# A new fixed order of the instructions on all five engines, chosen with VectorE's two-SBUF-input additions and GpSimd's instructions excluding each other

## The chip, the cores and the metric

The kernel runs on one core of one Trainium2 chip. The metric is device time in microseconds (us), the median of several runs; lower is better. A core has five engines with an instruction queue each: TensorE (PE, matmuls; its weight loads are shown apart as PEld), VectorE (DVE), ScalarE (ACT), GpSimd (POOL) and SyncE (SP). Here SyncE does nothing but issue the DMA transfers, all of them on one queue.

## The reference

Two identical layers, each of linear attention and a gated MLP, on 2048 rows of width 512 (32 heads of 16, MLP width 1792):

```python
def _A_ref(x, wqkv, wo):
    q, k, v = (x @ wqkv).reshape(B, S, 3, H, Dh).transpose(2, 0, 3, 1, 4)
    phi = lambda t: jnp.where(t > 0, t + 1, jnp.exp(t)) + 1e-6
    pq, pk = phi(q), phi(k)
    kv = jnp.einsum("bhsd,bhse->bhde", pk, v)
    z = jnp.einsum("bhsd->bhd", pk)
    num = jnp.einsum("bhqd,bhde->bhqe", pq, kv)
    den = jnp.einsum("bhqd,bhd->bhq", pq, z)[..., None] + 1e-6
    return (num / den).transpose(0, 2, 1, 3).reshape(B, S, D) @ wo

def _B_ref(x, w1, w3, w2):
    return (silu(x @ w1) * (x @ w3)) @ w2

for _ in range(2):
    x = x + _A_ref(_layernorm(x), A_wqkv, A_wo)
    x = x + _B_ref(_layernorm(x), B_w1, B_w3, B_w2)
```

## The kernel before

All matmuls run on fp16 pairs: every operand is split into a high and a low fp16 part, and a product takes three passes (high by high, low by high, high by low; `PASSES`). Large products are done as seven half-size products with 256 columns (a Winograd form), whose banks in PSUM are called bb, ba and bc in the MLP, kb, kc and ka for the keys of layer 2, qb, qc and qa for its queries. In layer 1 the keys have a bank pk and the Gram matrix of the rows gt; po is an output bank.

**Rows and tiles.** The 2048 rows are 16 tiles of 128. For each tile, VectorE takes the moments (L909 and L910, `bn_stats` and `bn_aggr`), GpSimd computes scale and shift in four or five small operations (L917 to L921, among them the power L918), ScalarE normalises (L924), ScalarE writes the high part and GpSimd or VectorE the low part, and a DMA transposes the pair (L939, L1858; in layer 2 L1590 and L1593 for the seven-product form). A copy of the transposed rows is stored in HBM (L1875, L1594) and loaded back later (L1888, L1685) for the queries. The first two tiles are transposed by TensorE instead (`turn`, L2355); their low parts are L2361.

**Scale of the weights.** Before the first product, VectorE takes the largest absolute value of four pieces of the key weights (L789), reduces these (L805), spreads the result over all partitions by a small matmul (`pm_k`, L808) and makes a power of two of it (L810 to L821). ScalarE and VectorE then split the weights by it (L836 high, L837 low).

**Layer 2, keys.** `pair_turn` handles two tiles at once: ScalarE L1586 and GpSimd L1587 (high), GpSimd L1588 and L1589 (low), transpose L1590; ScalarE L1591, GpSimd L1592, transpose L1593; store L1594 of 896 KB to xt7_d. **Layer 2, queries:** ScalarE L1717 and VectorE L1718, L1732 to L1753 make the features, ScalarE L1759 and GpSimd L1760 split them, a DMA transposes them (L1769), and po matmuls read them. ScalarE L1634 takes a product out of PSUM. L947 is the line of nearly all matmuls (the helper `mm`).

**What sets the order.** The kernel is written as a program, and at its end `arrange()` gives every engine a fixed order: the table `ORDER` holds for each engine the numbers of its instructions, as traced, in the order in which they shall run. Each instruction then depends on its predecessor on its own engine:

```python
for engine, text in ORDER.items():
    at = []
    for part in text.split():
        first, _, last_ = part.partition("-")
        at.extend(range(int(first), int(last_ or first) + 1))
    for before, after in zip(at, at[1:]):
        tc.add_manual_dep(traced[engine][after], traced[engine][before].name, ...)
```

The semaphores between engines follow from the data. SyncE's DMAs use eight semaphores in turn, so each DMA is issued only after the one eight places ahead of it has landed.

Of the kernel before, what the change touches and what calls it, by code (L numbers as in the profile page):

```python
# [73 lines left out]
        "0-20 22-23 26-27 24 28 25 30 29 34 38-39 35-36 21 31-32 37 40-41 33 42-65 78-89 66-77 "  # L74
        "102-113 90-92 96-101 93-95 126-137 120-122 114-116 123-125 117-119 150-161 144-149 "
        "162-173 138-140 174-176 183-185 141-143 180-182 177-179 186-197 201-203 198-200 204-209 "
        "228-230 225-227 210-224 231-245 258-269 255-257 249-254 246-248 276-278 282-293 279-281 "
        "306 300-302 307 303-305 308-319 270-272 326-328 273-275 294-299 323-325 350-352 347-349 "
        "329-331 353-355 332-343 320-322 377-379 344-346 356-367 380-391 404 371-373 405-406 "
        "374-376 398-400 368-370 401-403 395-397 392-394 416-418 407-409 413-415 419-421 410-412 "  # L80
        "425-427 431 422-424 428-430 432-455 460-471 456-458 472-483 459 484-555 568-579 556-567 "
        "592-603 616-627 580-591 604-615 628-651 664-675 652-663 688-699 676-687 712-723 700-711 "
        "736-747 760-771 724-735 748-759 772-808 821-832 809-820 833-868 893-904 869-880 905-910 "
        "917-928 881-892 911-916 941-958 965-970 929-934 1001-1006 935-940 971-976 959-964 "
        "1007-1012 977-988 1109 1013-1018 1049-1054 1110-1111 1085-1090 1019-1024 1112 1117-1120 "
        "1055-1060 989-994 1121 1113 1122 1114 995-1000 1115-1116 1373-1374 1125 1381 1126 1375 "
        "1091-1096 1376-1377 1382 1378 1383 1123-1124 1379 1384-1385 1380 1386 1037-1042 1387 "
        "1389 1388 1127 1393 1390 1128-1130 1394 1025-1030 1043-1048 1031-1036 1395 1061-1066 "
        "1131 1217-1218 1097-1102 1132 1391 1396 1219 1067-1072 1103-1108 1220 1225-1226 "
        "1073-1078 1221 1227 1392 1397-1399 1157-1162 1079-1084 1228-1229 1222 1230-1231 1223 "  # L90
        "1405 1163-1168 1224 1232 1237 1133-1138 1145-1150 1400 1233-1234 1406 1238 1151-1156 "
        "1235 1407 1236 1408-1409 1193-1204 1401 1239 1402 1169-1174 1139-1144 1175-1180 "
        "1410-1411 1403-1404 1413-1415 1205-1210 1325 1240 1416 1326 1265-1270 1327 1211-1216 "
        "1181-1186 1421 1333 1412 1422-1424 1328 1425 1329 1334 1187-1192 1417-1418 1335-1336 "
        "1330-1332 1419 1301-1306 1341 1337 1307 1338 1420 1339 1426 1429-1430 1308-1312 1340 "
        "1431 1345 1432 1346 1433 1253-1264 1271-1276 1241-1246 1427 1434 1342 1435-1436 1441 "
        "1347 1428 1343 1348 1437-1438 1344 1247-1252 1439 1277-1288 1313-1318 1442-1443 "
        "1505-1506 1319-1324 1445-1450 1507 1444 1481-1486 1440 1289-1300 1451-1456 1508 1513 "
        "1349-1354 1509-1510 1769 1511 1514 1512 1777 1521 1515-1520 1522 1770-1771 1523 1772 "
        "1525 1773 1526 1361-1366 1778-1779 1524 1355-1360 1367-1372 1457-1462 1780 1774 1781 "  # L100
        "1613 1775 1782 1487-1492 1776 1783 1614-1615 1784-1785 1463-1468 1493-1498 1786-1787 "
        "1789 1788 1790 1616 1527 1791 1793 1792 1469-1474 1794 1475-1480 1499-1504 1617 1528 "
        "1621-1623 1553-1558 1624 1801 1625-1627 1529-1534 1618 1541-1546 1619 1559-1564 1620 "
        "1628 1535-1540 1629-1630 1547-1552 1795 1633-1634 1796-1798 1802-1805 1589-1594 1635 "
        "1799 1806-1807 1800 1809 1565-1570 1631 1810 1632 1808 1811-1812 1595-1606 1571-1576 "
# [64 lines left out]
        "3752-3757 3819-3820 3734-3745 3821-3822 3831 3823-3828 3857-3862 3791-3796 3803-3808 "  # L170
        "3817-3818 3833 3797-3802 3809-3814 3829 3835 3832 3848-3849 3834 3830 3836-3837 "
        "3863-3868 3838-3839 3844-3847 3840-3841 3856 3850 3842-3843 3854 3852 3855 3853 3851 "
        "3869-3874 3917-3918 3893-3898 3875-3880 3921-3924 3899-3904 3881-3886 3905-3910 "
        "3887-3892 3911-3916 3925-3926 3962-3967 3933 3919-3920 3931 3927-3928 3935 3929-3930 "
        "3968-3973 3998-4002 3937 3934 3950-3961 4034-4035 3938-3943 4042 4026-4029 4003 "
        "3944-3949 3932 3974-3979 4038-4039 4022-4023 3936 4024-4025 3980-3985 4030-4031 "
        "4067-4070 4036-4037 4081 4032-4033 4004-4009 3986-3991 4010-4015 4040-4041 4082 "
        "4088-4089 3992-3997 4071-4076 4083 4079-4080 4016-4021 4077-4078 4109-4114 4090-4091 "
        "4087 4084 4145-4150 4102 4092-4093 4115-4120 4055-4060 4151-4156 4061-4066 4094-4095 "
        "4100-4101 4121-4126 4085 4108 4104-4105 4157-4162 4103 4127-4132 4043-4048 4086 "  # L180
        "4169-4170 4163-4168 4133-4138 4096-4097 4139-4144 4049-4054 4098-4099 4106 4214-4219 "
        "4173-4174 4220-4225 4250-4255 4171-4172 4107 4190-4195 4202-4213 4175-4176 4185 4183 "
        "4177-4178 4181-4182 4189 4184 4274-4275 4286-4287 4226-4231 4196-4201 4179-4180 "
        "4256-4261 4232-4237 4276-4277 4262-4267 4186 4278-4279 4288 4280-4281 4187 4290 4294 "
        "4289 4291 4188 4238-4249 4268-4273 4319-4320 4282-4285 4323-4324 4321-4322 4292 "
        "4333-4334 4340-4341 4293 4325-4326 4307-4312 4327-4328 4335-4336 4313-4318 4295-4300 "
        "4331-4332 4342-4343 4354 4301-4306 4382-4387 4329-4330 4355 4388-4393 4412-4417 "
        "4337-4338 4348-4349 4339 4352-4353 4350-4351 4344-4345 4358 4360 4359 4394-4405 "
        "4346-4347 4356-4357 4406-4411 4361-4362 4365-4366 4487-4492 4363-4364 4481-4486 "
        "4367-4368 4375 4369-4370 4377 4373-4374 4376 4371-4372 4418-4421 4432-4433 4381 "  # L190
        "4379-4380 4426-4427 4430-4431 4438 4378 4428-4429 4422-4425 4434 4436 4435 4439-4440 "
        "4437 4499-4504 4493-4498 4441-4446 4517-4522 4455-4456 4464-4465 4447-4448 4511-4516 "
        "4453 4466-4467 4454 4476 4449-4450 4460-4461 4457-4458 4468-4469 4477 4470-4471 "
# [2264 lines left out]
```

## Time and profile before

| | |
|---|---|
| median of 3 runs | 1137.82 us (1136.44 to 1138.37) |
| span of the profiled execution | 1134.0 us |
| instructions in the span | 22473 |
| TensorE busy | 1123.7 us (99%), 9117 matmuls |
| VectorE / ScalarE / GpSimd busy | 849.3 / 663.2 / 429.7 us |
| DMA moved | 162.94 MB, mean 144 GB/s |

The profile is of one execution; its only time is its span, which the median of the runs exceeds by 3.8 us. In the profile's rows, the first number is the start in us from the span's start, the second the duration; "L947" is a line of the kernel, "out<-in" the operands by the program's names (most SBUF tiles are parts of one large buffer, `arena`), and "[0.30 <-DMA arena<-arena]" at a row's end says how long the engine had stood idle before it and what ended the wait. "SPq" is SyncE's queue.

### The profile page before, as it was taken

How to read it: one execution, taken by the hardware profiler on the slowest of the kernel's cores; microseconds unless marked ns; L12 is line 12 of the kernel's file. 1: busy time of each engine (PE TensorE's matmuls, PEld its weight loads, DVE VectorE, ACT ScalarE, POOL GpSimd, SP SyncE). 2: the span in 40 equal slices, each digit the busy share in tenths (PEclk: the TensorE clock that was granted, in tenths of full speed). 3: DMA queues.
4: the chain of work that ended last, by engine and by line, in shares of the span. 5: the costliest groups of instructions: out<-in, count | busy, mean ns of one | idle time of the engine just before them, and what ended most of it. 6: DMA issues, size and time to landing. Idle time of an engine off the chain costs nothing.

```text
span 1134.0 us, 22473 instructions
## 1 busy us (share of the span) xinstructions
PE 1123.7 (99%) x9117; PEld 888.3 (78%) x9117; DVE 849.3 (75%) x1468; ACT 663.2 (58%) x1104; POOL 429.7 (38%) x477
## 2 busy tenths in 40 slices
PE   8999999999999999999999999999999999999998
PEld 3445446888888888888886676578888888888887
DVE  7789878896978887889896488847855666465556
ACT  7668878775544445455578666686544434343442
POOL 6731796502001222335678416862152110302113
PEclk9999999999999999999999999999999999999999
DMA  8995665389673332331267946643482440220001
GB/s 258 304 292 181 174 136 121 75 220 272 204 279 122 117 149 103 112 155 66 48 179 177 276 165 153 114 89 105 120 240 102 177 178 1 85 84 29 11 20 57
DMA packets 171768, 162.94 MB, mean 144 GB/s; under 512 B 139536, under 2 KB 147984, under 8 KB 167056
## 3 DMA queue, kind: packets, MB, share of 16 engines
q1 hardware_dynamic: 171664, 161.51, 48.7%
q8 instruction: 71, 1.16, 0.4%
q14 instruction: 33, 0.27, 0.1%
HBM read 80.08 MB, written 47.32 MB: 112 GB/s over the span
## 4 chain that ended last, share of the span: by engine, by line
PE 91%; DVE 2%; POOL 2%; DMA 2%; issue 1%; ACT 1%; SPq 0%; DVEq 0%; POOLq 0%; ACTq 0%
PE bb L947 26%; PE po L2097 20%; PE bc L947 13%; PE ba L947 6%; PE gt L947 6%; PE po L947 5%; PE pq L947 4%; PE pk L947 3%; PE po L2117 3%; DMA arena<-arena 2%; PE kb L947 1%; PE qb L947 1%; PE kc L947 1%; PE kv L947 0%; PE qc L947 0%
## 5 line engine op out<-in xcount | busy, mean ns | idle before, releaser
L947 PEld LDWEIGHTS <-arena 128*128 128x128 f16 x6648 | 646.1, 98 | 204.5 <-DMA arena<-arena 4.4
L947 PE MATMUL bb<-arena 128*128 128x256 f16 x2688 | 349.2, 273 | 0.0
L2097 PE MATMUL po<-arena 128*128 128x256 f16 x2058 | 288.5, 273 | 0.0
L2052 ACT ACTIVATE arena<-bb 128x512 f32<-128x512 f32 x196 | 115.3, 594 | 195.5 <-PE bb L947 166.7
L2097 PEld LDWEIGHTS <-arena 128*128 128x128 f16 x2058 | 201.3, 98 | 23.4
L947 PE MATMUL bc<-arena 128*128 128x256 f16 x1344 | 179.6, 273 | 0.0
L2055 DVE TENSOR_TENSOR arena<-arena,bc 128x512 f32<-128x512 f32 x112 | 76.7, 685 | 87.5 <-PE bc L947 54.1
L2007 ACT ACTIVATE arena<-arena,scalars 128x512 f32<-128x512 f32 x112 | 74.6, 666 | 90.2 <-DVE arena L2055 70.2
L2146 DVE SCALAR_TENSOR_TENSOR arena<-po,scalars,arena 128x256 f32<-128x256 f32 (+1 forms) x180 | 101.5, 585 | 31.7 <-PE po L2097 21.7
L2013 DVE TENSOR_TENSOR arena<-arena 128x1280 f16<-128x1280 f32 (+1 forms) x90 | 105.4, 1174 | 21.2 <-ACT arena L2011 20.8
L2011 ACT ACTIVATE arena<-arena 128x512 f16<-128x512 f32 (+1 forms) x112 | 101.0, 904 | 32.2 <-DVE arena L2026 13.7
L2008 DVE SCALAR_TENSOR_TENSOR arena<-arena,scalars 128x512 f32<-128x512 f32 x112 | 78.6, 705 | 34.5 <-ACT arena L2007 34.4
L947 PE MATMUL ba<-arena 128*128 128x256 f16 x672 | 91.8, 273 | 0.0
L947 PE MATMUL gt<-arena 128*128 128x512 f16 x384 | 89.6, 379 | 0.0
L947 PE MATMUL po<-arena 128*128 128x512 f16 x384 | 86.8, 379 | 0.5 <-DMA arena<-arena 0.5
L2013 POOL TENSOR_TENSOR arena<-arena 128x512 f16<-128x512 f32 x22 | 27.0, 1228 | 115.0 <-ACT arena L2011 108.2
L2155 POOL TENSOR_TENSOR arena<-arena 128x512 f32<-128x512 f32 x27 | 38.0, 1406 | 81.7 <-DVE arena L2146 81.7
L2154 POOL TENSOR_TENSOR arena<-arena 128x512 f32<-128x512 f32 x27 | 37.1, 1375 | 71.4 <-DVE arena L2146 69.3
L871 DVE SCALAR_TENSOR_TENSOR arena<-arena,scalars 128x512 f16<-128x512 f32 (+2 forms) x74 | 59.1, 814 | 2.3 <-ACT arena L869 2.2
L924 ACT ACTIVATE arena<-arena,nb_all,rs_all 128x512 f32<-128x512 f32 x64 | 50.8, 806 | 13.2 <-POOL nb_all L921 7.6
L2023 POOL TENSOR_TENSOR arena<-arena 128x256 f32<-128x256 f32 x10 | 7.9, 786 | 131.3 <-DVE arena L2008 131.3
L869 ACT ACTIVATE arena<-arena,scalars 128x512 f16<-128x512 f32 (+2 forms) x74 | 52.2, 718 | 5.2 <-DVE arena L1003 2.3
(234 smaller groups left out, 1449.4 us busy)
## 6 DMA issues: line engine op xcount, KB each, us to landing
arena<-xb_d SPq DMA_DIRECT2D x12, 1792.0 KB, 8.0
xb_d<-arena SPq DMA_DIRECT2D x8, 1792.0 KB, 7.7
w_d<-arena SPq DMA_DIRECT2D x5, 1792.0 KB, 7.6
arena<-w_d SPq DMA_DIRECT2D x5, 1792.0 KB, 8.0
arena<-in_B_w_dram SPq DMA_DIRECT2D x8, 896.0 KB, 7.0
arena<-in_B_w_dram SPq DMA_DIRECT2D x28, 256.0 KB, 3.0
xt_d<-arena SPq DMA_DIRECT2D x8, 896.0 KB, 5.1
arena<-xt_d SPq DMA_DIRECT2D x8, 896.0 KB, 6.7
```

What stands on the lines that cost most here:

```text
L869: nc.scalar.activation(hi, src, AF.Copy, scale=scale)
L871: lambda: nc.vector.scalar_tensor_tensor(lo, src, scale, hi, OP.mult, OP.subtract)
L924: nc.scalar.activation(dst, x_sb[:, t, :], AF.Identity, scale=rs_all[:, t : t + 1], bias=nb_all[:, t : t + 1],)
L947: nc.tensor.matmul(dst, lhs(a, k), rhs(b, k), start=first and k == 0 and i == 0, stop=last and k == n - 1 and i == len(PASSES) - 1, skip_g ...
L2007: nc.scalar.activation(t, gate, AF.Silu, scale=info["u1"])
L2008: nc.vector.scalar_tensor_tensor(t, up, info["hid"], t, OP.mult, OP.mult)
L2011: nc.scalar.activation(hs[:, 0, lo:hi], t[:, lo:hi], AF.Copy)
L2013: engine.tensor_tensor(hs[:, 1, lo:hi], t[:, lo:hi], hs[:, 0, lo:hi], OP.subtract)
L2052: nc.scalar.activation(dst, bank_, AF.Copy)
L2055: nc.vector.tensor_tensor(dst, dst, bank_, OP.add)
L2097: nc.tensor.matmul(po[:, i * HALF : (i + 1) * HALF], hs[:, a, qx, cs], w2[:, b, qw, :], start=g == ends[0] and i + a + b == 0, stop=g == e ...
L2146: nc.vector.scalar_tensor_tensor(dst, src, cb, to, OP.mult, OP.add)
```

## The change

Only the table `ORDER` differs. All five engines get a new order; the instructions, their operands, their buffers and their number stay. 959 of TensorE's 9100 entries stand at another place (moved by at most 27 places), 366 of VectorE's 1436 (at most 46), 284 of ScalarE's 1051 (at most 95), 191 of GpSimd's 475 (at most 25) and 92 of SyncE's 307 (at most 18). By the words that came with the change, the new order was chosen with a rule that VectorE's additions of two SBUF inputs and GpSimd's instructions shut each other out. TensorE's order differs in the stretches that ran before at 10 to 13, 26 to 60, 196 to 198, 506 to 663, 683 to 723 and 1089 to 1126 us.

```diff
@@ -71,38 +71,39 @@
 ORDER = {
     "PE": (
-        "0-20 22-23 26-27 24 28 25 30 29 34 38-39 35-36 21 31-32 37 40-41 33 42-65 78-89 66-77 "
-        "102-113 90-92 96-101 93-95 126-137 120-122 114-116 123-125 117-119 150-161 144-149 "
...
+        "0-20 22-27 30 28-29 34 38-39 21 35 31-32 36 40 37 41 33 42-65 78-89 66-77 102-113 "
+        "93-95 99-101 96-98 126-137 90-92 114-116 150-161 117-119 123-125 120-122 162-173 "
...
```

The table is seven lines longer, so that line numbers in the rows of the changed kernel are higher by seven (L1858 is L1865, L962 is L969, L918 is L925, L1588 is L1595, and so on).

**SyncE at the start.** The three loads of rows of x at the head of the queue (L2319) keep their place, but the second and the third change places with each other. Then follow four pieces of weights and more rows of x. A little later (the rows of issues from 19 to 34 us of before), before: L1858 are the transposes of a tile's rows, L962 a 896 KB piece of the MLP weight w1, L1875 the copies to HBM, L2319 rows of x, and the lines L2324 and L2326 attention weights.

```order
8 L1858 DMA_TRANSPOSE arena<-arena 128x8x128
9 L962 DMA arena<-in_B_w_dram 128x1792
10 L1875 DMA xt_d<-arena 128x1024
11 L1858 DMA_TRANSPOSE arena<-arena 128x8x128
12 L2319 DMA arena<-in_A_x_dram 128x512 x2
13 L1875 DMA xt_d<-arena 128x1024
14 L2319 DMA arena<-in_A_x_dram 128x512
15 L1858 DMA_TRANSPOSE arena<-arena 128x8x128
16 L2319 DMA arena<-in_A_x_dram 128x512
17 L1875 DMA xt_d<-arena 128x1024
18 L1858 DMA_TRANSPOSE arena<-arena 128x8x128
```

Now, in the same place (the lines seven higher):

```order
9 L1865 DMA_TRANSPOSE arena<-arena 128x8x128
10 L2326 DMA arena<-in_A_x_dram 128x512
11 L1882 DMA xt_d<-arena 128x1024
12 L2326 DMA arena<-in_A_x_dram 128x512
13 L1865 DMA_TRANSPOSE arena<-arena 128x8x128
14 L1882 DMA xt_d<-arena 128x1024
15 L1865 DMA_TRANSPOSE arena<-arena 128x8x128
16 L1882 DMA xt_d<-arena 128x1024
17 L969 DMA arena<-in_B_w_dram 128x1792
18 L2333 DMA arena<-in_A_wqkv_dram 128x512
19 L1865 DMA_TRANSPOSE arena<-arena 128x8x128
```

The w1 piece that stood between the first and the second of these transposes stands behind the third now, with a piece of the attention weights behind it, and ahead of the fourth. The second w1 piece also goes ahead of the transpose that follows it (issued at 38.97 us before).

**GpSimd in the keys of layer 2.** The two pairs of tiles whose rows of before run from 611 to 628 us; L917 to L921 are the small operations on the next tiles' moments, L1654 and L1655 two copies of scalars:

```order
297 L1592 TENSOR_TENSOR arena<-arena 128x1024
298 L1654 COPY arena<-scalars 128x2
299 L917 TENSOR_SCALAR ve<-mv_all 128x2
300 L920 TENSOR_SCALAR neg<-mv_all 128x2
301 L1588 TENSOR_TENSOR arena<-arena 128x512
302 L918 TENSOR_TENSOR rs_all<-ve,minus_half 128x2
303 L1587 CAST arena<-arena 128x2x256
304 L1589 TENSOR_TENSOR arena<-arena 128x2x256
305 L921 TENSOR_TENSOR nb_all<-neg,rs_all 128x2
306 L1592 TENSOR_TENSOR arena<-arena 128x1024
```

Now:

```order
286 L1599 TENSOR_TENSOR arena<-arena 128x1024
287 L924 TENSOR_SCALAR ve<-mv_all 128x2
288 L927 TENSOR_SCALAR neg<-mv_all 128x2
289 L925 TENSOR_TENSOR rs_all<-ve,minus_half 128x2
290 L1662 COPY arena<-scalars 128x2
291 L928 TENSOR_TENSOR nb_all<-neg,rs_all 128x2
292 L1595 TENSOR_TENSOR arena<-arena 128x512
293 L1662 COPY arena<-scalars 128x2
294 L1594 CAST arena<-arena 128x2x256
295 L1596 TENSOR_TENSOR arena<-arena 128x2x256
296 L1599 TENSOR_TENSOR arena<-arena 128x1024
```

The power (L918, now L925) and the product behind it (L921, now L928) went from between the pair's subtractions to ahead of the first of them.

**SyncE in the keys of layer 2.** The queue from 579 to 595 us of before; L1685 (now L1692) is the load of the first pair for the queries:

```order
151 L1590 DMA_TRANSPOSE arena<-arena 128x12x128
152 L1594 DMA xt_d<-arena 128x3584
153 L1593 DMA_TRANSPOSE arena<-arena 128x16x128
154 L1594 DMA xt_d<-arena 128x3584
155 L1685 DMA arena<-xt_d 128x3584
156 L1590 DMA_TRANSPOSE arena<-arena 128x12x128
```

Now:

```order
149 L1601 DMA xt_d<-arena 128x3584
150 L1692 DMA arena<-xt_d 128x3584
151 L1597 DMA_TRANSPOSE arena<-arena 128x12x128
152 L1601 DMA xt_d<-arena 128x3584
153 L1600 DMA_TRANSPOSE arena<-arena 128x16x128
154 L1601 DMA xt_d<-arena 128x3584
155 L1597 DMA_TRANSPOSE arena<-arena 128x12x128
```

The load went ahead of a pair's two transposes and two stores. In the queries, TensorE's block of twelve po matmuls that ran from 702.8 us on stands ahead of two groups of six qb and six qc matmuls now, which ran at 700.4 and 701.5 us before.

637 rows, old and new, of the table ORDER are left out of this document.

## The prediction

> **What bounds the kernel now.** I read the page's first part, then TensorE's waits, then the engines' busy time by stretches of the span, and only then the chain that ended last, at the places where the waits lie.
>
> ```profile
> span 1134.0 us, 22473 instructions
> PE 1123.7 (99%) x9117; PEld 888.3 (78%) x9117; DVE 849.3 (75%) x1468; ACT 663.2 (58%) x1104; POOL 429.7 (38%) x477
> ```
>
> TensorE (PE) is busy in 1123.7 of 1134.0 us. No matmul is added or removed, so an order of the same instructions can only take from the other 10.3 us. The profiled execution has no time of its own beside its span; the median of the three runs is 1137.82 us, so 3.8 us lie outside the span, and I take them as unchanged.
>
> ```profile
> PE turn L2355 <- POOL arena L2361: 2.2, 1, 2.2
> PE warm L2369 <- DVE scalars L732: 1.1, 1, 1.1
> PE kb L947 <- DMA arena<-arena: 0.8, 1, 0.8
> PE kc L947 <- DMA arena<-arena: 0.6, 1, 0.6
> PE po L947 <- DMA arena<-arena: 0.5, 1, 0.5
> ...
> PE pk L947 <- DMA arena<-arena: 0.3, 1, 0.3
> PE qc L947 <- ACT arena L1634: 0.3, 1, 0.3
> ```
>
> Columns: total, number, longest (us). Each wait is a single event, so each can be found in the order and followed.
>
> ```profile
> 0.00:50.00 50.00, 45.86 (x211) 20.55 (x212) 36.90 (x82) 37.30 (x60) 33.24 (x87) 1.00 0.96 283
> 600.00:650.00 50.00, 48.55 (x333) 32.10 (x332) 26.19 (x43) 36.90 (x49) 31.23 (x36) 1.00 0.84 227
> 700.00:750.00 50.00, 49.15 (x307) 29.67 (x305) 34.39 (x57) 36.33 (x70) 42.79 (x38) 1.00 0.56 106
> ```
>
> The first busy column is TensorE's; the last two are the DMA engines' share and GB/s. TensorE stands still for 4.14 us in the first 50, for 1.45 us in 600 to 650 and for 0.85 us in 700 to 750; what is left of the 10.3 lies almost whole in the tail behind the last matmul, where the chain stays. Of the start the 1.1 us of the row on warm come before the first possible matmul. The most that a new order can bring is about 4.14 - 1.1 + 1.45 + 0.85 = 5.3 us, 0.5% of the time. VectorE, ScalarE and GpSimd are not bounds over the span; they count only where they feed one of these waits.
>
> **Start, first matmuls.**
>
> ```profile
> 13.67 7.54 PE pk L947 x34
> 21.21 1.54 PE gt L947 x8
> 22.75 6.49 DMA arena<-arena
> 29.24 0.05 issue
> 29.29 2.76 PE pk L947 x12
> ```
>
> Columns: start, duration. Ahead of these rows the chain runs through an x load, VectorE's statistics L909, GpSimd's small operations per tile (L917 to L921), its subtraction L2361, the transposing matmuls, ScalarE L836 and VectorE L837; then come pk matmuls at 0.22 us each (7.54 / 34). The tile whose statistics hold GpSimd came third in the queue and now comes second.
>
> ```profile
> 5.60 0.69 DVE L909 BATCH_NORM_STATS2 st<-arena 128x6 f32<-128x512 f32 x1 [1.21 <-DMA arena<-in_A_x_dram]
> 7.51 2.49 DVE L789 TENSOR_REDUCE parts<-arena 128x1 f32<-128x512 f32 x4 [0.21 <-DMA arena<-in_A_wqkv_dram]
> arena<-in_A_x_dram SPq DMA_DIRECT2D x1, 256.0 KB, 2.9
> ```
>
> The second load is issued at 1.24 and takes 2.9, so it lands at 4.1 instead of 5.6: statistics, small operations and L2361 come up to 1.3 us earlier. The path then runs into VectorE's four reductions L789 of the weights, which end at 10.00 in the row above and are re-sorted to the order of landing; one reduction less behind the last landing lets L805 start about 0.5 us earlier. Two more 0.06 to 0.18 us operations now stand inside the scalar chain behind it. Between 0.5 (weights bind) and 0.9 us (they do not) I take 0.7. Against it stands a lock:
>
> ```profile
> 6.87 0.57 POOL L918 TENSOR_TENSOR rs_all<-ve,minus_half 128x1 f32<-128x1 f32 x1
> 12.99 1.04 POOL L918 TENSOR_TENSOR rs_all<-ve,minus_half 128x1 f32<-128x1 f32 x1
> ```
>
> GpSimd's L918 took 0.57 us alone and 1.04 where it began just after VectorE's first L837, which has two SBUF inputs. With the chain earlier, L918 comes just ahead of the first L837 and may hold it for a part of 0.57, at most 0.5; I take 0.1. Term A: -0.6 (from -0.9 to 0). The Trainium skill, "SBUF — State Buffer", section "SBUF: two separate sides", says that whichever of the two starts first keeps the shared ports for the whole instruction; the two rows agree. By that rule the hold here would be about 0.3, and the sum 0.2 us worse.
>
> **Start, the queue.** The wait at 29.29 ends with a transpose issued at 22.75, which needed 6.49 us because a 896 KB w1 load (L962) went out at 20.65.
>
> ```profile
> 28.48 1.24 SPq L1858 DMA_TRANSPOSE arena<-arena  x1
> arena<-in_B_w_dram SPq DMA_DIRECT2D x1, 896.0 KB, 6.1
> arena<-arena SPq DMA_TRANSPOSE x1, 4.2
> arena<-arena SPq DMA_TRANSPOSE x1, 7.5
> ```
>
> (The answers on the w1 load at 20.65, on the transpose at 31.41 and on the one at 59.38; the last number is us to landing.) That load now goes behind three transposes, so the wait goes. A wait costs more than its row: the rows count a matmul's modelled end, 0.38 us, while the next starts after 0.22, so 0.3 + 0.16 = 0.46. Term B: -0.46. But the load, and a second one behind it, is now ahead of the transposes that went out at 31.41 and 38.97. The first of these feeds a pk block that stands six matmuls earlier now: from 29.29 less the gains (1.1) and three matmuls moved (0.65), plus 39 x 0.22, it is due at about 36.1. The load goes out right behind the transpose of 28.48, about 29.3 in the new time; with its 6.1 it lands at 35.4, the transpose 0.9 behind it at 36.3. By the kindest row (4.2, issue 30.5) it lands at 34.7, with no wait; by the harshest (7.5) at 38.0, 1.9 late. I take 0.3.
>
> **Keys of layer 2, 570 to 645.**
>
> ```profile
> 604.46 0.14 POOL arena L1654
> ...
> 615.50 0.66 PE kc L947 x6
> 616.15 0.81 PE kb L947 x6
> ...
> 620.99 1.45 POOL arena L1588
> 622.44 1.72 POOL rs_all L918
> ...
> 628.23 5.18 DMA arena<-arena
> ```
>
> Here GpSimd leads: its subtractions end, the queue issues a transpose, and TensorE waits for the landing (kb, kc). For kc, the power L918 (1.72) stood inside the chain; now it is in front of L1588, where GpSimd waited for ScalarE. That is 1.3 us or more earlier at the transpose of 628.23, so the 0.6 + 0.16 = 0.76 go whole. For kb, L1654 (0.14) and the even smaller L921 leave the chain: 0.25 of its 0.8 + 0.16 = 0.96. The 0.81 for six kb matmuls at 616.15 against 0.66 is a hole of 0.15 that the waits do not list; three such in this stretch get a gt block to cover them, of which I count 0.3. Against it: the 896 KB load L1685 moves from behind the pair's store to ahead of a transpose.
>
> ```profile
> 580.74 1.43 SPq L1590 DMA_TRANSPOSE arena<-arena  x1
> 586.66 0.38 PE L947 MATMUL kb<-arena 128*128 128x256 f16 x2
> arena<-arena SPq DMA_TRANSPOSE x1, 6.0
> ```
>
> The first row is that transpose, the second its reader, 5.9 us later; the third is the answer on the transpose at 687.70, which went out right behind such a load and took 6.0. A new wait of 0 to 0.8 (the load a little earlier or the gains before it), I take 0.2. Term C: -0.76 - 0.25 - 0.3 + 0.2 = -1.1 (from -1.8 to -0.3).
>
> **Queries, 683 to 745.** Twelve po matmuls (2.6 us) now run before the qb and qc that waited for ScalarE L1634: 0.3 + 0.16 = 0.46 go.
>
> ```profile
> 730.42 3.24 DMA arena<-arena
> ```
>
> The po wait behind this landing (0.5 + 0.16 = 0.66) ends a chain over ScalarE, VectorE, GpSimd L1760 and the transpose, of which no link is taken out; reordering VectorE brings it 0.1 to 0.5 us forward. If the chain cannot follow the earlier TensorE, all of 0.46 comes back here; I take -0.5 for both places (0 to -1.1). Term D: -0.5.
>
> **No cost.** The reorders at 196, 506 to 569, 646 to 663 and in the last MLP (1090 to 1126): TensorE shows no wait there, the operands it takes earlier are resident, and the covers (matmul blocks of 2 us and more) remain. One is thin: at 659 a VectorE L1778 goes behind another of its operations and may cost 0.3; I count 0.1.
>
> **Sum.** -0.6 - 0.46 + 0.3 - 1.1 - 0.5 + 0.1 = -2.3. After 740 TensorE never waits up to its last matmul, so nothing given back is expected there. 1137.82 - 2.3 = 1135.5; the uncounted holes of 0.15 between short blocks would add some tenths, and I say 1135.3.
>
> **Rivals.**
> 1. Half is given back: the transposes behind the w1 load come 1.0 late instead of 0.3 and the po wait at 734 grows by what was gained. 2.3 - 0.7 - 0.5 = 1.1: 1136.7 us. For it: 0.96 DMA share in the start row, and no link taken out of the po chain.
> 2. Everything listed goes, with no new wait: 0.9 + 0.46 + 1.8 + 1.1 = 4.3, 1133.5 us. For it: each wait is a single event; against: it needs every thin landing to hold.
> 3. Slower: the queue at the start. If the transposes behind the moved loads take 7.5 instead of 4.2, the first is 1.9 late, the next, with a second 896 KB load in front, adds about 2, and the ones behind two more loads (due near 52 and 67) 1 to 2: some 5.3 us lost against the 2.6 that the sum gains without its 0.3: 1140.5 us. It decides once these landings are together more than 2.6 us late. Against: the row that took 7.5 had two such loads ahead of it, this one has one.
> 4. Nothing measurable: the waits only change names; 1137.8.
>
> **Numbers.** A change under 0.2% (2.28 us) is one that this measurement hardly tells from none. The bound lies at 1135.5, so the forecast has cases on both sides of it: 0.48 in all, 0.38 below and 0.10 above. Rival 2: 0.12, rival 1: 0.23, rival 4: 0.08, rival 3: 0.09. Faster: 0.38 + 0.12 = 0.50; within: 0.10 + 0.23 + 0.08 = 0.41; slower: 0.09. The range goes from rival 2 with the uncounted holes, 1133.2, to 1138.4, rival 4 with the upper end of the three runs' spread; outside lie rival 3 and the rims of rivals 2 and 4, not over 0.2.
>
> **What would show it.** Right: first pk matmul near 12.3 instead of 12.9; no DMA wait of pk near 28; no kc wait near 632; no qc wait near 700; start stretch at 46.7 to 47.2 busy. Wrong: a new pk wait for a DMA between 33 and 45; a kb wait near 585; a po wait over 0.8 near 732; any DMA wait of pk near 67.

## The result: 0.6% slower, and the profile after

The changed kernel takes 1144.01 us (median of five runs, 1142.75 to 1144.59) against 1137.82 (five runs, 1135.86 to 1138.76): a ratio of 1.0060, 95% interval 1.0048 to 1.0072. (Here and below, the ratio is estimated from all runs of both kernels. The quotient of the two medians can differ from it by up to 0.001; here it is 1.0054.) The forecast was 1135.3 with a range to 1138.4: the time moved the other way and lies outside the range.

The first part of the page and TensorE's waits of the changed kernel, to be read beside the first two fences of the prediction (columns of the waits: total, number, longest, us):

```profile
span 1142.8 us, 22461 instructions
PE 1126.4 (99%) x9117; PEld 888.6 (78%) x9117; DVE 857.7 (75%) x1468; ACT 665.0 (58%) x1106; POOL 432.2 (38%) x477
```

```profile
PE kb L954 <- ACT arena L1641: 2.2, 3, 1.0
PE pk L954 <- DMA arena<-arena: 2.2, 2, 2.0
PE bb L954 <- ACT arena L2059: 1.6, 2, 0.8
...
PE bc L954 <- DVE arena L2062: 0.9, 1, 0.9
PE po L954 <- DVE arena L1757: 0.9, 1, 0.9
PE ba L954 <- DVE arena L1960: 0.8, 1, 0.8
...
PE kc L954 <- DMA arena<-arena: 0.2, 1, 0.2
```

The waits that the change aimed at are gone or small: kb for a DMA (0.8 before) and qc for ScalarE (0.3) are no longer listed, kc fell from 0.6 to 0.2. The pk wait at 29 is gone too. In their place stand waits of kb for ScalarE, of bb, bc and ba (banks of the MLP) for ScalarE and VectorE, and of pk for a DMA at other times. ScalarE has 1106 instructions instead of 1104; the table of its instructions shows what the two are, further down.

TensorE's busy time by stretches, of the changed kernel and, in the second fence, one of the kernel before (the second number is TensorE's, the third from the end its granted clock):

```profile
0.00:50.00 50.00, 46.42 (x207) 20.73 (x208) 34.88 (x80) 36.65 (x58) 33.96 (x83) 0.97 0.91 274
50.00:100.00 50.00, 47.83 (x226) 22.47 (x225) 45.16 (x81) 34.42 (x58) 15.11 (x28) 1.00 0.82 226
150.00:200.00 50.00, 49.07 (x265) 25.69 (x264) 40.36 (x76) 38.21 (x83) 41.38 (x41) 1.00 0.59 117
...
750.00:800.00 50.00, 49.20 (x428) 41.56 (x427) 30.41 (x53) 39.38 (x72) 22.71 (x24) 1.00 0.41 98
```

```profile
50.00:100.00 50.00, 50.00 (x236) 23.64 (x235) 43.67 (x85) 34.20 (x57) 14.03 (x23) 1.00 0.79 231
```

TensorE now stands still for 3.6 us in the first 50 and 2.2 in the next, and for 0.8 to 1.5 in each of the seven stretches of 50 us from 150 to 250 and from 550 to 800: 12.5 us in all. Before, it did so for 6.4, all of it in the three stretches that the prediction showed; in 50 to 100 it never stopped, as the row has it, nor in 150 to 250, 550 to 600, 650 to 700 and 750 to 800. The two profiles differ by 8.8 us in span: 6.1 of them are TensorE's idle time (16.4 against 10.3), and 2.7 are busy time (1126.4 against 1123.7). Of these 2.7, about 1.7 (an estimate: half of 3.4) come from 3.4 us of matmuls at half the clock at the start of this execution (the last section). The timed difference is smaller, 6.2. The profiled execution of before was a short one: in every run of the experiments the time is 1.7 to 1.8 us above the span, so that execution took about 1135.8, 2.0 below the median. The profiled execution of the changed kernel took 1144.59, 0.6 above its median. The 3.8 us that the prediction put outside the span were therefore wrong, without weight for its difference.

### The profile page after: what moved, and what is told of

The parts are those of the page before. It is cut to its first block, busy times and chain, and to the rows that moved or that the text cites. A ratio compares the mean times of both kernels' runs of the same rounds, so it can differ in the third digit from the quotient of the medians.

```text
span 1142.8 us, 22461 instructions
## 1 busy us (share of the span) xinstructions
PE 1126.4 (99%) x9117; PEld 888.6 (78%) x9117; DVE 857.7 (75%) x1468; ACT 665.0 (58%) x1106; POOL 432.2 (38%) x477
## 4 chain that ended last, share of the span: by engine, by line
PE 73%; DVE 3%; ACT 3%; POOL 1%; issue 1%; DMA 0%; POOLq 0%; DVEq 0%; ACTq 0%
PE bb L954 25%; PE po L2104 19%; PE bc L954 12%; PE ba L954 6%; PE po L2124 3%; PE gt L954 3%; PE kb L954 1%; PE po L954 1%; PE qb L954 1%; DVE arena L1739 1%; PE kc L954 1%; ACT arena L1965 1%; DVE arena L1742 0%; PE qc L954 0%; DMA arena<-arena 0%
## 5 line engine op out<-in xcount | busy, mean ns | idle before, releaser
L2014 ACT ACTIVATE arena<-arena,scalars 128x512 f32<-128x512 f32 x112 | 74.5, 666 | 82.2 <-DVE arena L2062 59.6
L878 DVE SCALAR_TENSOR_TENSOR arena<-arena,scalars 128x512 f16<-128x512 f32 (+2 forms) x74 | 62.2, 853 | 2.8 <-ACT arena L876 2.7
```

Of the source, the lines that this page charges most:

```text
L878: lambda: nc.vector.scalar_tensor_tensor(lo, src, scale, hi, OP.mult, OP.subtract)
L2014: nc.scalar.activation(t, gate, AF.Silu, scale=info["u1"])
```

## Experiments

**In which places the time was lost.** Four kernels keep the order of before except in one stretch of the program. There all five engines take the new order.

```diff
 # ORDER[engine] = old list up to the stretch + list of the stretch + old list behind it
-list of the stretch: old
+e1_start: new, instructions that ran up to 100 us
+e2_mlp1:  new, 157 to 206 us (end of the layer's attention, first MLP begins)
+e3_keys:  new, 495 to 640 us
+e4_query: new, 640 to 760 us
```

> The new order only in the first 100 us, the order of before in the rest. Theory of places (each new wait of TensorE belongs to the order in its own stretch): +3.4 us in the span, as TensorE's matmuls run 3.4 us later at 100 us in the changed kernel: the first pk matmuls at half the clock (+1.0 after the earlier start), two waits of 0.3 for transposes, one of 2.1 for the transpose read at 85 us, less the 0.5 of the wait at 29. Rival (phases: the waits only arise from how the DMA queue happened to stand in the profiled execution): within 1 us of before.

> The new order only in the stretch from 157 to 206 us (end of the first attention, first groups of the first MLP). Theory of places: +3.0 us, from three waits of bc, ba and bb of 0.9 to 1.1 us behind VectorE and ScalarE. Rival (the waits need the delays that the start brought in): within 0.5 us of before.

> The new order only from 495 to 640 us (last groups of the first MLP, keys of layer 2). Theory of places: -1.6 us in the span: the waits of 1.0 at 613 and half of the 0.8 at 633 go, small holes too, one of 1.1 at 586 behind ScalarE L1634 comes. Rival (phases): between -0.5 and +0.5.

> The new order only from 640 to 760 us (end of the keys, queries of layer 2, start of the second MLP). Theory of places: +4.1 us: waits of kb for ScalarE L1634 (0.7 and 0.9), gt (0.3), the po wait at 733 grown from 0.7 to 1.2, a bb wait of 1.0 at the end. Rival (phases): within 1 us.

Measured against 1136.95 of before: e1_start 1138.72, ratio 1.0018 (1.0008 to 1.0028); e2_mlp1 1139.45, 1.0018 (1.0009 to 1.0027); e3_keys 1137.63, 1.0008 (0.9999 to 1.0016); e4_query 1138.99, 1.0021 (1.0012 to 1.0030). Three of the four places are slower by themselves, and the keys bring nothing. Of the four, the prediction had given a loss to none. The sum of the four, 0.65%, agrees with the 0.60% of the whole change within the intervals, as separate losses would; the rest of the order, the last MLP above all, was not run by itself. The theory of places, which read the losses off one profile, got the signs of three places but not the sizes: +3.4, +3.0 and +4.1 us were expected, and about 2 each came. In the keys it expected -1.6, and the median rose by 0.7.

One more thing is in the runs. Of the twelve runs of e2_mlp1, ten took 1138.4 to 1140.3 us and two 1135.2 and 1135.5, below the median of before. The same fixed order can lose time in one execution and not in another (see the end of the attention, below).

**A table load on ScalarE.** ScalarE's rows of the changed kernel:

```profile
647.99 1.28 ACT L1843 ACT_TABLE_LOAD   x1
649.28 0.20 ACT L1843 ACTIVATE scalars<-scalars 128x1 f32<-128x1 f32 x1
...
649.96 1.28 ACT L1683 ACT_TABLE_LOAD   x1
651.25 1.06 ACT L1683 ACTIVATE arena<-arena 128x1024 f32<-128x1024 f32 x1
```

L1843 (L1836 of before) is an activation of one element with the function Silu, `nc.scalar.activation(idle, one_eps, AF.Silu)`. Its only use is to have the table of Silu in place before the second MLP. Before, it ran at 733 us, behind the last exponential. The new order puts it at 649 us, between two exponentials (L1683): the table goes to Silu, back for the next exponential, and to Silu again at the MLP. ScalarE's instructions grouped by line, first of after and then of before, show the loads but for two at the start that both have (columns behind the bar: busy us, mean ns, idle time ahead):

```profile
L1683 ACT ACT_TABLE_LOAD x2 | 2.6, 1283 | 0.0
...
L1843 ACT ACT_TABLE_LOAD x1 | 1.3, 1283 | 0.0
L2014 ACT ACT_TABLE_LOAD x1 | 1.3, 1283 | 0.0
```

```profile
L1676 ACT ACT_TABLE_LOAD x1 | 1.3, 1283 | 0.0
L1836 ACT ACT_TABLE_LOAD x1 | 1.3, 1283 | 0.0
```

Four loads became six. Those at 648 and 650 make kb wait, the one ahead of L2014 at 762 makes bb wait. The first test moves this one activation back in the kernel with the new order from 640 to 760 us; the second does the same in the whole changed kernel. ScalarE's order, first kernel (L1837 and L1677 are L1836 and L1676 of before):

```diff
 L1676 ACTIVATE arena<-arena,scalars 128x1024
-L1837 ACT_TABLE_LOAD
-L1837 ACTIVATE scalars<-scalars 128x1
 L1635 ACTIVATE arena<-kb,scalars 128x256
-L1677 ACT_TABLE_LOAD
 L1677 ACTIVATE arena<-arena 128x1024
...
 L1958 ACTIVATE nm_all<-total 128x1
+L1837 ACT_TABLE_LOAD
+L1837 ACTIVATE scalars<-scalars 128x1
```

> The run before with the new order from 640 to 760 us, but one ScalarE instruction back where it was: the activation of one element with Silu (L1836) that the new order took from 733 to 643 us, between two exponentials. Theory of the table: two of the three table loads of 1.28 us in this stretch go, with them the kb waits of 0.3 and 0.9, the gt wait of 0.3 near 645 and the bb wait of 1.0 near 759: span 2.0 to 2.5 us below the 1136.6 of the run with the whole stretch, a time within 0.5 us of before. Rival (the many other ScalarE moves do it): at most 0.5 us less than that run.

> The whole new order with one ScalarE instruction back where it was, the Silu of one element (L1836). Theory of the table: 1.5 to 2.5 us less than the changed kernel, a ratio to before of 1.0038 to 1.0048, with four table loads in place of six. Rival (the other moves in the queries cost as much without it): a ratio of 1.0055 or more.

e5_silu took 1137.40 against 1136.74, 1.0008 (0.9999 to 1.0017), where the same stretch with the early Silu had 1.0021. e9_after_silu took 1140.58 against 1137.01, 1.0033 (1.0020 to 1.0046), where the whole change has 1.0060. TensorE in 640 to 690 and 750 to 800 us, e4_query first, then e5_silu:

```profile
640.00:690.00 50.00, 49.08 (x374) 34.66 (x373) 35.15 (x56) 34.52 (x50) 8.57 (x8) 1.00 0.62 196
750.00:800.00 50.00, 49.19 (x443) 43.18 (x442) 34.69 (x62) 36.61 (x61) 17.74 (x18) 1.00 0.48 110
```

```profile
640.00:690.00 50.00, 50.00 (x389) 35.90 (x387) 33.76 (x57) 29.95 (x44) 10.52 (x12) 1.00 0.67 212
750.00:800.00 50.00, 50.00 (x448) 43.49 (x446) 34.87 (x61) 36.96 (x63) 19.70 (x20) 1.00 0.44 103
```

TensorE's 0.92 and 0.81 us of idle time vanish with the two loads. One entry of some 1900 moved ones costs about 0.13% in its stretch, and on the point estimates nearly half of the change's loss (0.27 of 0.60%, about 3 us). The second figure is more than the 1.5 to 2.5 us of the theory. The profile of e9_after_silu also lacks the waits at 190 to 206 us, which this entry does not explain, so not all of the 0.27% need be the tables. In these rows the load begins 0.02 us behind the instruction ahead of it, and the next instruction 0.01 behind the load: a switch takes 1.3 us of ScalarE. The Trainium skill, "ScalarE: Activation LUTs", section "What ACT_TABLE_LOAD costs", has the same 1283 ns for the load and adds a drain of about 1380 ns to it; no row here shows that drain.

**The queue at the start.** The wait at 84 to 86 us (2.0 us, the longest new one) ends with a transpose. SyncE's issues in the changed kernel:

```profile
58.96 0.43 SPq L969 DMA_DIRECT2D arena<-in_B_w_dram  x1
...
67.50 0.56 SPq L969 DMA_DIRECT2D arena<-in_B_w_dram  x1
68.18 0.84 SPq L1882 DMA_DIRECT2D xt_d<-arena  x2
75.23 1.24 SPq L1865 DMA_TRANSPOSE arena<-arena  x1
76.51 0.58 SPq L969 DMA_DIRECT2D arena<-in_B_w_dram  x1
...
77.68 2.16 SPq L1865 DMA_TRANSPOSE arena<-arena  x1
```

One of the two copies at 68.18 stood, before, ahead of the 896 KB load that now goes out at 58.96. It lies behind two such loads now, and these copies take 6.5 us to land (first row below). The transpose at 75.23 writes where that copy reads, so it goes out only then; the load behind it slips from 68.26 to 76.51 and falls directly in front of the transpose of 77.68. The same transpose and load before:

```profile
66.97 1.24 SPq L1858 DMA_TRANSPOSE arena<-arena  x1
68.26 0.58 SPq L962 DMA_DIRECT2D arena<-in_B_w_dram  x1
```

How long the copies at 68.18 and the transpose at 77.68 took, and in the second fence the latter in the kernel before, where it was issued at 75.21 (the last number is us to landing):

```profile
xt_d<-arena SPq DMA_DIRECT2D x2, 256.0 KB, 6.5
arena<-arena SPq DMA_TRANSPOSE x1, 7.8
```

```profile
arena<-arena SPq DMA_TRANSPOSE x1, 3.0
```

The test moves this one copy back in e1_start:

```diff
 L962 DMA arena<-in_B_w3_dram 128x1792
-L1858 DMA_TRANSPOSE arena<-arena 128x8x128
-L962 DMA arena<-in_B_w3_dram 128x1792
-L1875 DMA xt_d<-arena 128x1024 x2
+L1875 DMA xt_d<-arena 128x1024
+L1858 DMA_TRANSPOSE arena<-arena 128x8x128
+L962 DMA arena<-in_B_w3_dram 128x1792
+L1875 DMA xt_d<-arena 128x1024
```

> The new order in the first 100 us with one SyncE instruction back where it was: the store of a transposed tile (L1875), which the new order put behind two 896 KB loads. Theory of the chain in the queue: the transpose that overwrites the stored tile goes out near 67 in place of 74 us, the w1 load behind it near 68 in place of 75, and the transpose issued at 77 lands in 3 to 4.5 us in place of 7.6: the pk wait at 84 us (0.9, in the changed kernel 2.1) goes. The waits at 45 and 54 us stay. Rival (the queue is full there anyhow): the wait at 84 keeps at least 0.5.

1135.96 against 1137.01, 0.9995 (0.9987 to 1.0004), where e1_start had 1.0018. The wait at 84 is gone. A part of the difference may be the clock at the start (last section), whose mean over the span was under 1.000 in 6 of the 8 runs of e1_start and in 2 of these 11; among the others, the medians are 1137.62 (two runs) and 1135.71 (nine). Two others stay, TensorE's rows with a DMA ahead of them:

```profile
44.02 2.76 PE L947 MATMUL pk<-arena 128*128 128x512 f16 x12 [0.60 <-DMA arena<-arena]
53.20 2.76 PE L947 MATMUL pk<-arena 128*128 128x512 f16 x12 [1.24 <-DMA arena<-arena]
```

They belong to transposes that have 256 KB loads of attention weights ahead of them. The next test starts from e10_store and puts three of these loads behind the transposes:

```diff
-L2326 DMA arena<-in_A_wqkv_dram 128x512
 L2324 DMA arena<-in_A_wqkv_dram 128x512
 L1875 DMA xt_d<-arena 128x1024 x2
 L1858 DMA_TRANSPOSE arena<-arena 128x8x128 x2
+L2326 DMA arena<-in_A_wqkv_dram 128x512
 L2326 DMA arena<-in_A_wo_dram 128x512
 L1875 DMA xt_d<-arena 128x1024 x2
+L1858 DMA_TRANSPOSE arena<-arena 128x8x128 x2
 L2326 DMA arena<-in_A_wqkv_dram 128x512 x2
-L1858 DMA_TRANSPOSE arena<-arena 128x8x128 x2
```

> The new order in the first 100 us with the store put back, and three 256 KB loads of attention weights (L2326) put behind the transposes that they stood ahead of. Theory of the queue: the pk waits at 44 and 53 us (0.8 and 1.4) go as well; 1.5 to 2.2 us under the 1134.9 of the run with the store alone, ratio to before 0.998 to 0.999. Rival (the 896 KB load of w1 is what holds the first of the two): the wait at 44 keeps at least 0.4.

1139.32 against 1136.79, 1.0017 (1.0008 to 1.0026), where 0.998 to 0.999 was expected. The two waits go, and others come: of gt for GpSimd L1366 at 59 us (0.3), of pm_v (a small matmul in the scaling of the weights) for VectorE L805 at 66 (0.5), of gt for VectorE L1405 at 68 (0.4), and of pk for a DMA at 70 (0.7). The one of pm_v fits weights that are now late. The profiled execution was the fastest of the eleven (1137.14), so the waits that make up the other 2.2 us of the median were not seen.

Another test, of the whole queue, gives the engines their new order at the start and SyncE its old one; it told less:

```diff
 # e1_start, ORDER["SP"]
-new list up to 100 us
+old list up to 100 us
```

> The new order in the first 100 us on TensorE, VectorE, ScalarE and GpSimd, SyncE's queue as before. Theory of the queue: the waits for transposes at 45, 54 and 84 us (0.4, 1.0, 0.9) go and the one at 29 us (0.5) comes back: +0.5 us against before in place of +1.8. Rival (the loss is the matmuls at half clock, 1.5 us, from the idle stretches ahead of them): about +1.5, with the granted clock under 1.00 again in the start.

1142.25, 1.0058 (1.0045 to 1.0071), far above both +0.5 and +1.5 us. Its longest new waits are gt for GpSimd L1366 (1.7) and for VectorE L1405 (1.3 in four). The reading that the engines' new order takes the tiles in another sequence than the old queue brings them was not tested. The run does not say what the new queue costs; it says that queue and engines cannot be exchanged apart.

**End of the attention, 157 to 206 us.** VectorE's and GpSimd's rows of the changed kernel:

```profile
185.91 1.22 DVE L878 SCALAR_TENSOR_TENSOR arena<-arena,scalars 128x512 f16<-128x512 f32 x1
187.05 2.10 DVE L1933 TENSOR_SCALAR den<-den 128x32 f32<-128x32 f32 x1
186.88 2.24 POOL L2001 TENSOR_TENSOR arena<-arena 128x1024 f16<-128x1024 f32 x1 [0.29 <-ACT arena L1995]
```

L1933 has a single SBUF input and 32 elements per partition. In the kernel before it took 0.18 us:

```profile
183.02 0.18 DVE L1926 TENSOR_SCALAR den<-den 128x32 f32<-128x32 f32 x1
```

Here L878, moved in front of it, makes it start 0.17 us behind GpSimd's L2001, and it ends at 189.15 where L2001 ends at 189.12. So a small operation of one input is held for the whole GpSimd instruction too, which the rule named in the change, for additions of two inputs, does not cover. The Trainium skill, "SBUF — State Buffer", section "Who interferes with whom", says that `tensor_scalar`, like copies and casts, can run in VectorE modes that use the ports shared with GpSimd where its operands allow it, and that whichever of the two engines issues first then has them for its whole instruction; the rows agree with it. Whether this hold makes the bc wait (and the loss) was tested by moving that L871 (L878 of after) back in e2_mlp1, and by giving ScalarE or VectorE its whole old list in this stretch:

```diff
 # e7_l871 against e2_mlp1, VectorE
 L1953 SCALAR_TENSOR_TENSOR arena,total<-po,scalars,arena 128x512
+L871 SCALAR_TENSOR_TENSOR arena<-arena,scalars 128x2x256
 L1930 TENSOR_TENSOR arena<-pq,den 128x512
...
 L1911 TENSOR_REDUCE den<-pq 128x32
-L871 SCALAR_TENSOR_TENSOR arena<-arena,scalars 128x2x256
 L1926 TENSOR_SCALAR den<-den 128x32
 # e13_actold, e14_dveold against e2_mlp1, 157 to 206 us
-ORDER["ACT"] new      -ORDER["DVE"] new
+ORDER["ACT"] old      +ORDER["DVE"] old
```

> The new order from 157 to 206 us with one VectorE instruction back where it was: the L871 that the new order put between the reduction L1911 and the small L1926. Theory of the lock: without it L1926 is issued before GpSimd's long L1994 begins and is not held 1.9 us; the bc wait of 1.2 near 189 goes; the two later waits (0.9 each) have their own causes and stay or shrink: 1.2 to 2 us less span than the 1138.6 of the run with the whole stretch. Rival (VectorE is simply full there): the bc wait keeps at least 0.6.

> The new order from 157 to 206 us on every engine but ScalarE, which keeps the order of before. If ScalarE's moves (L836 ahead of L2007, L1988 and L924 ahead of the copies out of PSUM) make the loss: ratio to before 1.0000 to 1.0008, and no bb wait near 202. If VectorE's moves with GpSimd's lock make it: 1.0015 to 1.0022 as in the run with the whole stretch, with the bc wait near 189.

> The new order from 157 to 206 us on every engine but VectorE, which keeps the order of before. If VectorE's moves with GpSimd's lock make the loss: 1.0000 to 1.0008, L1926 at 0.2 us again and no bc wait near 189. If ScalarE's moves make it: 1.0015 to 1.0022, with the bb wait near 202.

e7_l871: 1138.63, 1.0023 (1.0013 to 1.0032). L1926 takes 0.18 again, and in its profile the bc wait is gone and the ba wait with it; waits of bb for ScalarE stay (1.0 in two). The ratio does not fall against the 1.0018 of e2_mlp1; against their own runs of before, the median is 0.6 us lower, and the intervals do not tell the two apart. e13_actold: 1138.91, 1.0021 (1.0012 to 1.0029), with a bb wait for ScalarE of 1.1. e14_dveold: 1138.72, 1.0014 (1.0006 to 1.0023). Here L1926 starts 0.76 behind the GpSimd instruction and takes 1.40; in e13_actold it starts together with it and takes 0.17:

```profile
184.27 2.13 POOL L1994 TENSOR_TENSOR arena<-arena 128x1024 f16<-128x1024 f32 x1 [0.31 <-ACT arena L1988]
185.03 1.40 DVE L1926 TENSOR_SCALAR den<-den 128x32 f32<-128x32 f32 x1
```

```profile
185.63 0.17 DVE L1926 TENSOR_SCALAR den<-den 128x32 f32<-128x32 f32 x1
```

The hold is thus shown as a mechanism, and the bc wait goes with it. But L871's place does not decide it: e14_dveold has VectorE's old list and the hold, e13_actold the new one and none. Two profiles of other experiments say the same. In e5_silu, whose order is the old one up to 640 us, the same instruction takes 1.47 us, and a bc wait of 0.7 comes. In e9_after_silu, which has the whole new order here, it takes 0.17, and TensorE stands still for 0.06 us in 100:

```profile
150.00:200.00 50.00, 50.00 (x275) 26.83 (x274) 40.17 (x81) 40.40 (x86) 42.42 (x41) 1.00 0.61 123
200.00:250.00 50.00, 49.94 (x458) 44.62 (x457) 45.66 (x73) 37.15 (x68) 14.57 (x17) 1.00 0.53 120
```

So the waits of this stretch depend on how an execution arrives there as well as on the order. As the cause of the time the hold is not shown: neither ScalarE's nor VectorE's list carries the 0.18% alone. TensorE's, GpSimd's and SyncE's new lists stayed in all three tests, and what carries the loss stays open.

**Keys.** In the stretch from 495 to 640 us, the wait of kb for a DMA at 613 goes as forecast, and a new one of kb for ScalarE comes at 586. The chain that ended last, in the changed kernel:

```profile
581.75 1.15 ACT arena L1682
...
583.28 1.28 ACT L1683
...
584.57 1.06 ACT arena L1683
585.63 0.46 ACT arena L1641
...
586.13 0.82 PE kb L954 x6
```

L1641 (L1634 of before), which frees the bank, ran at 572.87 ahead of these in the old order; the matmul now waits for two long activations and a table load that have nothing to do with it. Moving it back (e3_keys, ScalarE; L1632 is L1634 of before, L1674 is L1676):

```diff
 L2009 ACTIVATE arena<-arena 128x1280
+L1632 ACTIVATE arena<-kb,scalars 128x256
 L1632 ACTIVATE arena<-kb,scalars 128x256
 L1673 ACTIVATE arena<-arena,scalars 128x1024
...
 L1674 ACTIVATE arena<-arena 128x1024
-L1632 ACTIVATE arena<-kb,scalars 128x256 x2
+L1632 ACTIVATE arena<-kb,scalars 128x256
```

> The new order from 495 to 640 us with one ScalarE instruction back where it was: the L1634 that the new order put behind L1673 (the exponentials' line is L1676 before), L2146 and a table load. Theory of the queue of ScalarE: the kb wait of 1.1 near 579 goes and the gains at 613 and 633 us stay: span 1.1 us below the 1134.5 of the run with the whole stretch, and time 0.5 to 1 us below before. Rival: the wait turns up behind the next kb (0.5 or more of it stays).

1137.05, 1.0004 (0.9996 to 1.0013) against 1.0008 of e3_keys. The intervals do not tell the two apart. The wait of kb for ScalarE is gone, and another of nearly the same length comes (TensorE's waits of this kernel):

```profile
PE po L945 <- DMA arena<-arena: 1.1, 1, 1.1
...
PE po L2095 <- DVE arena L2144: 0.7, 1, 0.7
```

The po wait for VectorE L2144 at 582 is new. The one for a DMA at 734 (0.5 before) was 1.1 in e3_keys already.

**What was found, put back together.** The whole changed kernel, with four entries at their old places: the Silu, the copy to HBM, L871, and one ScalarE L836 ahead of the bb wait at 205.

```diff
 # whole new ORDER, four numbers back between their old neighbours
-SP: copy to HBM behind two w loads    -ACT: Silu at 649 us; L836 ahead of L2007
-DVE: L871 ahead of L1926
+SP: copy ahead of the second w load   +ACT: Silu at 733 us; L836 behind L2007
+DVE: L871 ahead of L1930
```

> The whole new order with four instructions back where they were: the Silu on ScalarE, the store of a transposed tile on SyncE, the L871 on VectorE at 186 us, and on ScalarE the L836 that stood ahead of L2007 near 202 us. Theory of single misplaced instructions: 4 to 5 us less than the changed kernel, a ratio to before between 1.0005 and 1.0025. Rival (the loss is spread over hundreds of moves): a ratio of 1.004 or more.

1139.52 against 1137.01, 1.0016 (1.0007 to 1.0024). On the point estimates, four moved entries carry 0.44 of the 0.60%. In its profile waits of pk at 37 and 54 us, of kb for ScalarE at 584 and of po at 738 remain, and of bb at 188 and 203: the L836 put back did not take the last one away.

**The clock at the start.** Some executions show the half clock in 12 to 16 us, others not, with either order. In e12_warm the order is that of before, and seven more matmuls on constants, whose output nothing reads, fill TensorE's idle time between 8 and 10.4 us. e16_best adds them to e15_loads.

```diff
-        keep_busy(22)
+        keep_busy(29)    # seven of them behind the first two turning matmuls
```

> The order of before with seven more warming matmuls in TensorE's idle stretch from 8.1 to 10.4 us; their output is not used. Theory of the clock: the half-clock stretch of 3.4 us at 12 us, which some executions show and others not, with both orders, goes with the idle ahead of it: granted clock 1.00 in the start, the runs nearer together (1135 to 1137 us), median 0.3 to 1 us below before. Rival (the dip has nothing to do with that idle): median within 0.3 us of before or above, the same spread.

> The run before with seven more warming matmuls ahead of the second group of transposing matmuls; their output is not used. If the two gains add up: ratio to before 0.997 to 0.9985, granted clock 1.00 in the start. If the new start order with its shorter idle stretch has no half-clock stretch to lose: as the run before, 0.998 to 0.999.

e12_warm took 1135.96 against 1137.01, 0.9991 (0.9983 to 1.0000), the only version whose interval does not reach above 1, and the lowest beside e10_store. The gain of 0.1% is less than what was called measurable above. The granted clock was below 1.000 over the span in 3 of its 11 runs and in 80 of the 121 of before. e16_best took 1139.54, 1.0029 (1.0018 to 1.0040), where 0.997 to 0.999 was expected. In its profile, of the slowest of the seven runs (1143.36), the clock stays at 1.00 up to 20 us, and three waits of pk for a DMA take 4.3 us in all. That an earlier TensorE only meets the same transposes sooner is a guess that no run tested.

## Why the prediction was wrong, point by point

**The paragraph "No cost" failed, and with it went about half of what the forecast missed.** It judged the reorders at 196 and 646 to 663 by TensorE alone ("TensorE shows no wait there, the operands it takes earlier are resident, and the covers (matmul blocks of 2 us and more) remain") and priced them at 0.1. e2_mlp1 and e4_query measured 0.18 and 0.21%, 2.0 and 2.4 us. That TensorE did not wait there said only that the old order of the other engines fed it in time; the new order of VectorE, ScalarE and GpSimd was what had to be looked at. At 649 us the Silu's table loads are shown to do it (e5_silu), and their place could be read from ScalarE's order before any run. At 157 to 206 us the waits for VectorE and ScalarE are seen, but which entries bring them stays open.

The other half lies in terms A to C. By the ratios the start came out 2.0 us slower where A and B gave -0.8, and the keys 0.9 slower where C gave -1.1.

**Term A, -0.6, did not come.** The second x load and its statistics came earlier as argued (L2368 starts at 8.34 instead of L2361's 9.24). But the weights bound the path. VectorE's rows in the changed kernel:

```profile
8.19 2.02 DVE L796 TENSOR_REDUCE parts<-arena 128x1 f32<-128x512 f32 x3 [0.67 <-DMA arena<-in_A_wqkv_dram]
10.24 0.16 DVE L812 TENSOR_REDUCE scalars<-parts 128x1 f32<-128x4 f32 x1
```

Three reductions run from 8.19 on, when a piece of the weights has landed, where before four ran from 7.51 on; so L812 starts at 10.24 against 10.04; the first pk matmul starts at 13.05, not at 12.3 (12.9 before). The lock that the term feared at the first L844 (L837 of before) shows in no row.

**Term B, -0.46 + 0.3.** The wait at 29 went, as said. The price of what moved behind the loads was the error: instead of 0.3 at one place, the waits at 45, 54 and 84 us take 0.3, 0.4 and 2.1 in start-to-start time of TensorE. The sum looked at the first load only. The copy that frees a transpose's target, and so shifts a whole row of issues by 8 us, was not followed. Rival 3 had transposes that come late behind the moved loads, and the sign, but other places and not the copy, and got 0.09; the copy put back turns 1.0018 into 0.9995.

**Term C, -1.1.** The gains were right in kind: kb's wait at 613 went whole, kc's fell to 0.2. The 0.2 for the load L1692 did not come, since kb does not wait for a DMA near 585. At that place it waits for ScalarE instead, 1.0 in the list of waits, so that the stretch as a whole gives 1.0008 in place of 0.999.

**Term D, -0.5.** The qc wait went. The po wait, which the term let shrink, is 0.9 instead of 0.5, as rival 1 had it ("no link taken out of the po chain"), and comes from VectorE now.

**The sum** of listed waits was sound as far as waits can be removed: most were. What was missing is the other side. The prediction's bound of 5.3 us on what a new order can bring had no counterpart for what it can cost, and the 0.09 for slower rested on one place. Two of its own signs of being wrong came true: a kb wait near 585 and a po wait over 0.8.

## What to carry to other kernels

Before crediting a new order with the waits it removes, go through every engine's moved entries where TensorE does *not* wait, and ask for each what it is now behind: a table load, a 896 KB load, a long instruction of the engine it shares a lock with. A one-element preload or a 256 KB copy can weigh more than hundreds of other moves (those of the keys cost nothing measurable), and it shows in the listing of the order. And expect a repaired wait to come back elsewhere: of five single repairs here, two gave time back (the Silu and the copy); the other three (L871, L1634, the weight loads) took their wait away, and no time was gained that the intervals show.

## What the runs showed of the hardware

**The half clock at the start comes and goes.** TensorE's busy time and granted clock in the same 4 us, first of the changed kernel, then of the kernel before:

```profile
12.00:16.00 4.00, 4.00 (x15) 1.76 (x14) 3.83 (x8) 3.94 (x7) 3.46 (x6) 0.57 1.18 279
```

```profile
12.00:16.00 4.00, 3.82 (x21) 1.71 (x19) 3.84 (x14) 3.60 (x7) 2.05 (x4) 1.00 0.96 265
```

In the first, the granted clock is halved for 3.4 us (an estimate from the 0.57 over these 4 us), and the pk matmuls in it start every 0.43 us instead of 0.22. In the nine profiles with the half clock TensorE was busy for 0.8 to 2.1 of the 4 us from 8 to 12; the nine without it had 1.4 to 3.7. Below 1.4 all had it, between 1.4 and 2.1 both occur, and the five profiles with 2.2 or more all kept the full clock. Five are few: three of the eleven runs of e12_warm, whose profile has 3.3, still show a granted clock under 1.000 over the span. Of the 121 runs of before that stood beside the experiments, 41 had a granted clock of 1.000 over the span and a median of 1136.77, 64 had 0.998 and 1137.05, 13 had 0.999 and 1136.21, and three had 0.997 and 1138.72. A price of the half clock on the kernel before cannot be told from these: some tenths at most between the two large groups. The Trainium skill, "TensorE: Matmul & The Clock Gate", section "What's actually happening", describes activity windows of about 3.4 us that do not start with the kernel, which fits both the length and the chance.

**A few tenths decide a hold.** L1926 (L1933 of after) took 0.17 us where it started together with GpSimd's instruction, and 2.10 and 1.40 where it started 0.17 and 0.76 us behind it. In the changed kernel that cost VectorE 1.9 us, for 32 elements a partition. It starts late by chance, too: with the old order in this stretch, e5_silu has it 0.69 us behind, and it takes 1.47.
